# GFNet mixing and SoLU on one core: an opening stage with other places for its weights, stores, evictions and row splits

## The chip, the cores and the metric

The kernel runs on one core of one Trainium2 chip. A profile is of one execution; its span is about 2 us shorter than the device time of the same execution. The granted clock is the share of TensorE's full clock that the throttle granted in a stretch, the DMA share the mean busy share of the 16 DMA engines.

## The reference, cut to what matters

```python
# x: (8, 3136, 256)  filt_r, filt_i: (1569, 256)  w_in: (256, 1024)  w_out: (1024, 256), weights in float64
X = np.fft.rfft(x, axis=1)
y = np.fft.irfft(X * (filt_r + 1j * filt_i), n=3136, axis=1)
h = y.reshape(25088, 256) @ w_in
e = np.exp(h - h.max(-1, keepdims=True))
solu = h * e / (e.sum(-1, keepdims=True) + 1e-9)
ln = (solu - solu.mean(-1, keepdims=True)) / np.sqrt(solu.var(-1, keepdims=True) + 1e-6) * g_ln
out = ln @ w_out
```

## The kernel before

The transform over 3136 = 49 x 64 points is done in steps of matmuls with a pass through device memory between them. For the first two entries of the batch (group 0) it stands ahead of the main part, but for the last step of entry 1; this is the opening. The rest is done in pieces between the blocks of the main part, where a block is 128 tokens through both weight matrices. The first eight blocks, in which TensorE still has to wait, are called the ramp.

The opening has three parts. In the first step, 16 pieces of x (98 rows x 1024) are loaded, multiplied (`pa`), evicted (copied) from PSUM, where matmuls leave their results, to `t` and stored to device memory `d`. In the unit loop, 25 units are fetched back, multiplied (`pb`), turned and multiplied with the filter (`i`, `p`), multiplied again (`pc`), evicted (`g`) and stored. On the way back, entry 0 is fetched again and multiplied in small matmuls of 98 columns (`py`).

```python
sp = Spectrum(0, pools, resident)
for i in range(2 * NH // NCH):                      # first step: 16 pieces
    sp.fetch_x(i)                                   # one transfer of 98 rows, from SyncE
    sp.first(i, (0, 1), ..., either)                # evictions in turn on ScalarE and VectorE
    sp.store_first(i, nc.scalar.dma_start)          # one transfer of 100 rows, from ScalarE
    if i < 3:
        load_group(i)                               # tables and filters of 5 units each
...
for i in range(NS):                                 # unit loop: 25 units
    sp.multiply(i)
    if i + 1 < NS:
        start(i + 1)                                # fetch in two transfers, filter, pb
    sp.inverse(i, nc.scalar.copy if i % 3 == 0 else nc.vector.tensor_copy)
    sp.store(i, nc.scalar.dma_start)
    if i in (6, 9, 12, 15):
        load_float64(...)                           # w_in: 10 VectorE instructions each
...                                                 # w_out: four more conversions, way back
with tc.manual_schedule():
    for k in range(blocks + LAG):                   # main part, one block each
        hidden(k)                                   # h, maximum (VectorE), exponential (ScalarE)
        ...
        for job in early[k]: job()                  # pieces of other entries: pa, py, pb
        ...                                         # project, normalize (square on ScalarE)
        for job in products[k] + late[k] + stores[k] + loads[k]: job()
```

## Time and profile before

| | before |
|---|---|
| device time, median (range) | 1905.72 us (1905.46 to 1908.1) |
| span of the profile | 1902.9 us |
| first product of the unit loop | 79.8 us |
| first matmul of the way back | 174.3 us |
| first and eighth hidden layer `h` | 203.4 us, 276.5 us |

The prediction below shows the slices, the windows and the waits.

### The profile page before, as it was taken

The page shows a single profiled execution, that of the slowest core. Times are in us where ns is not written, and L with a number is a line of the kernel's source. Part 1 is how long each engine was busy: PE and PEld are TensorE (multiplying, and loading weights), DVE is VectorE, ACT ScalarE, POOL GpSimd, SP SyncE. Part 2 cuts the span into 40 slices and gives each one's busy share as a digit, 9 for nine tenths or more (in the row PEclk, how much of TensorE's full clock was granted, in tenths as well). Part 3 has the DMA queues.
Part 4 walks back from the last instruction along what each step waited for, and adds up shares of the span by engine and source line. Part 5 has one row for each costly group of instructions (what it writes and reads, how often), then busy time and mean ns, then how long its engine had stood idle before and what let it go on. Part 6 is the DMA issues. An engine that isn't in the chain of part 4 may idle for free.

```text
span 1902.9 us, 21234 instructions
## 1 busy us (share of the span) xinstructions
PE 1823.8 (96%) x6500; PEld 1168.5 (61%) x6500; DVE 1137.0 (60%) x1815; ACT 791.5 (42%) x1297; POOL 440.7 (23%) x1293
## 2 busy tenths in 40 slices
PE   6677889999999999999999999999999999999997
PEld 1224546676666666666666666667677676666665
DVE  1597445567766655566766655566666565566663
ACT  1142344554555544444545434344444334333331
POOL 2010133343334311123333211123322010110110
PEclk9686799999999999999999999999999999999999
DMA  9675279986877866575776656557675545434444
GB/s 268 214 211 188 92 226 239 241 209 174 189 194 204 200 150 149 134 170 140 166 186 148 151 137 141 137 134 177 146 178 112 119 100 117 99 86 110 96 92 100
DMA packets 320399, 300.78 MB, mean 158 GB/s; under 512 B 28625, under 2 KB 286418, under 8 KB 320288
## 3 DMA queue, kind: packets, MB, share of 16 engines
q1 hardware_dynamic: 284624, 206.69, 46.3%
q0 software_dynamic: 26704, 79.63, 14.9%
q10 hardware_dynamic: 8960, 13.11, 2.3%
q8 instruction: 53, 0.87, 0.2%
q14 instruction: 58, 0.48, 0.1%
HBM read 118.44 MB, written 81.40 MB: 105 GB/s over the span
## 4 chain that ended last, share of the span: by engine, by line
PE 88%; DVE 4%; DMA 2%; issue 1%; ACT 1%; POOL 0%; ACTq 0%; DVEq 0%; SPq 0%; POOLq 0%
PE h L396 35%; PE po L456 35%; PE py L253 6%; PE pc L226 4%; PE pb L196 4%; PE pa L169 3%; DMA d<-t 1%; DVE p L217 1%; DVE i L216 0%; DVE p L215 0%; DVE g L229 0%; DMA t<-d 0%; DVE nmax L401 0%; DMA f<-f_dram 0%; DMA raw_in<-in_moe_w_in_dram 0%
## 5 line engine op out<-in xcount | busy, mean ns | idle before, releaser
L456 PE MATMUL po<-w_out_sb,solu_t 128*128 128x256 f32 x3136 | 711.0, 380 | 4.5 <-DVE ot L464 4.5
L396 PE MATMUL h<-w_in_sb,y 128*128 128x512 f32 x1568 | 713.4, 598 | 0.0
L456 PEld LDWEIGHTS po<-w_out_sb,solu_t 128*128 128x128 f32 x3136 | 591.0, 190 | 137.7 <-issue 58.1
L396 PEld LDWEIGHTS h<-w_in_sb,y 128*128 128x128 f32 x1568 | 296.2, 192 | 317.8 <-issue 306.7
L401 DVE TENSOR_REDUCE nmax<-h 128x1 f32<-128x1024 f32 x196 | 239.6, 1222 | 419.6 <-PE h L396 419.6
L404 ACT ACTIVATE e<-h,nmax 128x1024 f32<-128x1024 f32 x196 | 218.5, 1115 | 605.0 <-DVE nmax L401 605.0
L421 ACT ACTIVATE e<-solu,nmu 128x1024 f32<-128x1024 f32 x196 | 225.0, 1148 | 287.9 <-DVE solu L419 287.9
L419 DVE SCALAR_TENSOR_TENSOR solu<-e,rsum,h 128x1024 f32<-128x1024 f32 x196 | 250.9, 1280 | 7.1 <-DVE rsum L416 0.2
L429 DVE STREAM_TRANSPOSE turn<-solu 128x1024 f32<-128x1024 f32 x196 | 241.8, 1234 | 0.0
L235 POOL DMA_DIRECT2D d<-g x152 | 93.7, 621 | 507.5 <-ACT g L229 507.4
L253 PEld LDWEIGHTS py<-wi_t,t 100*128 100x128 f32 x1024 | 146.0, 211 | 51.1 <-issue 36.0
L169 PE MATMUL pa<-x,wf_t 98*100 98x512 f32 x256 | 148.5, 687 | 25.9 <-DMA x<-in_x_dram 12.5
L253 PE MATMUL py<-wi_t,t 100*128 100x98 f32 x1024 | 145.4, 293 | 6.7 <-DMA t<-d 3.5
L448 POOL COPY rs_t<-rs 32x1 f32<-32x1 f32 x784 | 141.7, 181 | 35.7
L464 DVE TENSOR_SCALAR ot<-po,rs_t 128x256 f32<-128x256 f32 x196 | 94.4, 482 | 80.5 <-PE po L456 74.2
L215 DVE TENSOR_TENSOR p<-pb,f 128x512 f32<-128x512 f32 (+1 forms) x101 | 69.0, 684 | 120.4 <-ACT i L208 119.3
L196 PE MATMUL pb<-t,de 128*128 128x512 f32 (+1 forms) x250 | 110.9, 544 | 19.2 <-DVE p L215 10.0
L226 PE MATMUL pc<-p,de 128*128 128x512 f32 (+1 forms) x250 | 110.0, 539 | 14.9 <-DVE p L217 11.5
L442 POOL TENSOR_SCALAR rs<-var 128x4 f32<-128x4 f32 x49 | 9.3, 189 | 445.7 <-ACT e L421 443.6
L169 PEld LDWEIGHTS pa<-x,wf_t 98*100 98x100 f32 x256 | 45.7, 188 | 94.5 <-issue 59.9
L196 PEld LDWEIGHTS pb<-t,de 128*128 128x128 f32 x250 | 47.8, 198 | 78.4 <-issue 43.5
L256 ACT COPY y<-py 128x392 f32<-128x392 f32 x112 | 93.6, 836 | 5.1 <-PE py L253 5.1
(62 smaller groups left out, 868.2 us busy)
## 6 DMA issues: line engine op xcount, KB each, us to landing
solu_t<-turn SPq DMA_DIRECT2D x784, 128.0 KB
t<-d SPq DMA_DIRECT2D x64, 400.0 KB
t<-d SPq DMA_DIRECT2D x198, 128.0 KB
x<-in_x_dram SPq DMA_DIRECT2D x64, 392.0 KB
out_dram<-ot SPq DMA_DIRECT2D x196, 128.0 KB
d<-t POOLq DMA_DIRECT2D x48, 400.0 KB, 5.6
d<-g POOLq DMA_DIRECT2D x148, 128.0 KB, 3.6
f<-f_dram POOLq DMA_DIRECT2D x104, 128.0 KB, 4.3
```

The costliest lines, as they stand in the source:

```text
L169: nc.tensor.matmul(out=ps[0:NK, j], lhsT=wf_t, rhs=self.xs[i][0:NR, 2 * u:2 * u + 2, :], start=True, stop=True)
L196: nc.tensor.matmul(out=ps[:, w * j:w * j + w, :], lhsT=de[:, s + j, 0, :], rhs=t2[:, w * j:w * j + w, :], start=True, stop=True)
L226: nc.tensor.matmul(out=ps[:, w * j:w * j + w, :], lhsT=de[:, s + j, 1, :], rhs=pt[:, w * j:w * j + w, :], start=True, stop=True)
L253: nc.tensor.matmul(out=psv[:, i, :], lhsT=t4s[e, ch][:, i, cb * P:cb * P + P], rhs=wi_t, start=True, stop=True)
L396: nc.tensor.matmul(out=h[:, half, :], lhsT=y[:, c, P * t:P * t + P], rhs=w_in_sb[:, c, 512 * half:512 * half + 512], start=(c == 0), stop= ...
L401: nc.vector.tensor_reduce(out=nmax, in_=h, axis=AX.X, op=ALU.max, negate=True)
L404: nc.scalar.activation(out=e, in_=h, func=AFT.Exp, bias=nmax, accum_out=esum)
L419: nc.vector.scalar_tensor_tensor(out=solu, in0=e, scalar=rsum, in1=hs.pop(k), op0=ALU.mult, op1=ALU.mult, accum_out=nmu)
L421: nc.scalar.activation(out=e, in_=solu, func=AFT.Square, bias=nmu, scale=-float(DFF), accum_out=variances[g][:, i:i + 1])
L429: nc.vector.transpose(out=turns[g][:, :, i, :], in_=solus.pop(k).rearrange("p (f j) -> p f j", j=32))
L448: nc.gpsimd.tensor_copy(out=rss[g][32 * i:32 * i + 32, c:c + 1], in_=rs[32 * c:32 * c + 32, i:i + 1])
L456: nc.tensor.matmul(out=ps, lhsT=solu_t[:, f, :], rhs=w_out_sb[:, f, :], start=(f == 0), stop=(f == KF - 1))
```

## The change

Its intent is to shorten the opening. VectorE is relieved in the unit loop: the conversion of w_in moves into the first step, that of w_out to the way back, and evictions go to ScalarE. The stores of the loop are issued from GpSimd. A unit is one transfer instead of two. Transfers of 98 or 100 rows are cut into 96 rows and a rest of 2 or 4, so that the large part is spread over more DMA engines. In the first six blocks, pieces of the other entries stand ahead of the hidden layer instead of behind it, and the last preparation of w_out moves into the first three blocks.

```diff
+    def by_16(dmas, out, in_):
+        n = out.shape[0] // 16 * 16
+        dmas[0](out=out[:n], in_=in_[:n])
+        dmas[1](out=out[n:], in_=in_[n:])
 # loads of x, stores of the first step, loads of the way back: by_16(...) instead of one transfer
 # fetch(i), store(i) of a unit: one transfer of 128 partitions instead of two of 64
         for i in range(2 * NH // NCH):
             sp.fetch_x(i)
-            sp.first(i, (0, 1), ..., either)
-            sp.store_first(i, nc.scalar.dma_start)
-            if i < 3:
-                load_group(i)
+            sp.first(i, (0, 1), ..., nc.scalar.copy)
+            sp.store_first(i, (nc.scalar.dma_start, nc.gpsimd.dma_start))
+            if i in (1, 4, 7):
+                load_tables(i // 3)
+            if i >= 8 and i % 2 == 0:
+                load_float64(weights[(i - 8) // 2][0], load_words(weights[(i - 8) // 2][1], i))
 ...
-            sp.inverse(i, nc.scalar.copy if i % 3 == 0 else nc.vector.tensor_copy)
-            sp.store(i, nc.scalar.dma_start)
-            if i in (6, 9, 12, 15):
-                load_float64(w_in_sb[...], ...)
+            sp.inverse(i, nc.scalar.copy)
+            sp.store(i, nc.gpsimd.dma_start)
 ...
-                (early, late)[u][t].append(lambda ...: sp.first(...))
+                (first_of if t < LAG else (early, late)[u])[t].append(lambda ...: sp.first(...))
 ...                                             # the same for back(...)
         for k in range(blocks + LAG):
+            for job in first_of[k]:
+                job()
             if k < blocks:
                 hidden(k)
 ...
+            if k < 3:
+                prepare_w_out(k)
```

(The core; the layout of the tables and of the device-memory buffers follows from it.)

More of the change, by code (lines that the diff above doesn't have):

```diff
@@ L58, in dft_tables @@
     v[0, :, 0], v[1, :, 0] = 1.0, 0.0
-    wf = np.zeros((N1, 2, 2, NS, 2))
-    wi = np.zeros((2, NS, 2, N1, 2))
+    wf = np.zeros((N1, 2, NS, 2, 2))
+    wi = np.zeros((NS, 2, 2, N1, 2))
     for h in range(2):
-        wf[:, h, :, :, h] = w
-        wi[:, :, h, :, h] = v.transpose(0, 2, 1) / S
+        wf[:, h, :, :, h] = w.transpose(0, 2, 1)
+        wi[:, :, h, :, h] = v.transpose(2, 0, 1) / S
     kap = np.where(q[:, None] < 32, s + N1 * q[:, None], s + N1 * (95 - q[:, None]))
@@ L108 @@
     small = pool("sm", 4)
-    d1 = [dram.tile([len(g[0]), 2 * NS, N2, C], FP32, name=f"d1_{n}") for n, g in enumerate(GROUPS)]
-    d2 = [dram.tile([len(g[0]), 2 * NS, N2, C], FP32, name=f"d2_{n}") for n, g in enumerate(GROUPS)]
+    d1 = [dram.tile([len(g[0]), NS, P, C], FP32, name=f"d1_{n}") for n, g in enumerate(GROUPS)]
+    d2 = [dram.tile([len(g[0]), NS, P, C], FP32, name=f"d2_{n}") for n, g in enumerate(GROUPS)]
     f_dram = dram.tile([NS, NQ, 2, C], FP32, name="f_dram")
@@ L120 @@
     neg_half = consts.tile([P, 4], FP32, name="neg_half")
+    ones = consts.tile([P, P], FP32, name="ones")
+    w_bar = consts.tile([P, C], FP32, name="w_bar")
     nc.vector.memset(neg_half, -0.5)
@@ L148, in __init__, with columns @@
             self.xs, self.t1s, self.t2s, self.fs, self.prods, self.gs = {}, {}, {}, {}, {}, {}
-        def rows(self, ap, s, count, p):
+        def columns(self, ap, s, count):
             if len(self.entries) == 2:
-                return ap[:, p * NS + s, :, :].rearrange("b n c -> n b c")
-            return ap[0, p * NS + s:p * NS + s + count, :, :].rearrange("s n c -> n s c")
+                return ap[:, s, :, :].rearrange("b p c -> p b c")
+            return ap[0, s:s + count, :, :].rearrange("s p c -> p s c")
         def fetch_x(self, i):
@@ L158, in fetch_x @@
             self.xs[i] = self.pools["r"].tile([P, NCH, C], FP32, name=f"x_{self.n}_{i}", tag="r")
-            nc.sync.dma_start(out=self.xs[i][0:NR],
-                              in_=x[self.entries[b]].rearrange("(r n) c -> r n c", n=NH)[
-                                  :, NCH * ch:NCH * ch + NCH, :])
+            by_16((nc.sync.dma_start, nc.sync.dma_start), self.xs[i][0:NR],
+                  x[self.entries[b]].rearrange("(r n) c -> r n c", n=NH)[
+                      :, NCH * ch:NCH * ch + NCH, :])
         def first(self, i, halves, ps, evac):
@@ L173, in first, with store_first @@
                  in_=ps[0:NK].rearrange("p a b -> p (a b)"))
-        def store_first(self, i, dma):
+        def store_first(self, i, dmas):
             b, ch = divmod(i, NH // NCH)
-            dma(out=d1[self.n][b].rearrange("a (h n) c -> (a h) n c", h=2)[
-                :, NCH * ch:NCH * ch + NCH, :], in_=self.t1s.pop(i))
+            by_16(dmas, d1[self.n][b].rearrange("s (a n) c -> (s a) n c", a=4)[
+                :, NCH * ch:NCH * ch + NCH, :], self.t1s.pop(i))
             del self.xs[i]
@@ L184, in fetch @@
             self.t2s[i] = self.pools["t2"].tile([P, 2, C], FP32, name=f"t2_{self.n}_{i}", tag="t2")
-            for p in range(2):
-                nc.sync.dma_start(out=self.t2s[i][N2 * p:N2 * p + N2, 0:cols, :],
-                                  in_=self.rows(d1[self.n], s, count, p))
+            nc.sync.dma_start(out=self.t2s[i][:, 0:cols, :],
+                              in_=self.columns(d1[self.n], s, count))
         def fetch_filter(self, i):
@@ L233, in store @@
             gt, cols = self.gs.pop(i), len(self.entries) * count
-            for p in range(2):
-                dma(out=self.rows(d2[self.n], s, count, p),
-                    in_=gt[N2 * p:N2 * p + N2, 0:cols, :])
+            dma(out=self.columns(d2[self.n], s, count), in_=gt[:, 0:cols, :])
     t4s = {}
@@ L243, in fetch_back @@
         t4s[e, ch] = rows_pool.tile([P, NCH, C], FP32, name=f"t4_{e}_{ch}", tag="r")[0:NK]
-        nc.sync.dma_start(
-            out=t4s[e, ch],
-            in_=d2[n][b].rearrange("a (h n) c -> (a h) n c", h=2)[:, NCH * ch:NCH * ch + NCH, :])
+        by_16(
+            (nc.sync.dma_start, nc.sync.dma_start), t4s[e, ch],
+            d2[n][b].rearrange("s (a n) c -> (s a) n c", a=4)[:, NCH * ch:NCH * ch + NCH, :])
     def back(e, ch, cb, evac):
@@ L256, in back, with psum @@
         evac(out=y[:, cb, t0:t0 + S].rearrange("p (r n) -> p n r", n=NH)[:, n0:n0 + NCH, :], in_=psv)
-    flip = [0]
-    def either(out, in_):
-        flip[0] ^= 1
-        if flip[0]:
-            nc.scalar.copy(out=out, in_=in_)
-        else:
-            nc.vector.tensor_copy(out=out, in_=in_)
+    def psum(kind, name):
+        return {"b": ps_b, "t": ps_t, "o": ps_o}[kind].tile([P, 2, C], FP32, name=name, tag=kind)
     with ExitStack() as st:
@@ L271, with load_words @@
         fpool = pool("fp", 3, stack=st)
-        wpool = pool("wp", 1, stack=st)
-        def load_float64(dst, src, n):
+        wpool = pool("wp", 2, stack=st)
+        def load_words(src, n):
             raw = wpool.tile([P, 512, 2], I32, name=f"raw_{n}", tag="raw")
@@ L280, in load_float64 @@
                 in_=src)
+            return raw
+        def load_float64(dst, raw):
             lo, hi = raw[:, :, 0], raw[:, :, 1]
-            power = wpool.tile([P, 512], I32, name=f"power_{n}", tag="power")
-            frac = wpool.tile([P, 512], I32, name=f"frac_{n}", tag="frac")
+            power = wpool.tile([P, 512], I32, name="power", tag="power", bufs=1)
+            frac = dst.bitcast(I32)
             ts, stt = nc.vector.tensor_scalar, nc.vector.scalar_tensor_tensor
@@ L297, in load_float64, with load_tables @@
             stt(out=rest, in0=lo, scalar=2.0 ** -44, in1=rest, op0=ALU.mult, op1=ALU.mult)
-            nc.vector.tensor_tensor(out=dst, in0=frac.bitcast(FP32), in1=rest, op=ALU.add)
-        groups = {}
-        def load_group(g):
+            nc.vector.tensor_tensor(out=dst, in0=dst, in1=rest, op=ALU.add)
+        filters = {}
+        def load_tables(g):
             gs = slice(NG * g, NG * g + NG)
             nc.gpsimd.dma_start(out=de[:, gs, :, :], in_=de_dram[:, gs, :, :])
-            groups[g] = f = fpool.tile([P, NG, 2, C], FP32, name=f"f_{g}", tag="f")
+            filters[g] = f = fpool.tile([P, NG, 2, C], FP32, name=f"f_{g}", tag="f")
             for k, filt in enumerate((filt_r, filt_i)):
@@ L309, in load_group @@
                                         in_=filter_rows(filt, half, NG * g, NG))
-                nc.vector.tensor_copy(out=f[NQ:P, :, k, :], in_=f[0:NQ, :, k, :])
+            nc.vector.tensor_copy(out=f[NQ:P], in_=f[0:NQ])
+        weights = []
+        for c in range(KD):
+            for half in range(2):
+                hs = slice(512 * half, 512 * half + 512)
+                weights.append((w_in_sb[:, c, hs], w_in_words[P * c:P * c + P, hs]))
+        for h in range(4):
+            weights.append((w_out_sb[:, 2 * h:2 * h + 2, :].rearrange("p k d -> p (k d)"),
+                            w_out_words[256 * h:256 * h + 256].rearrange("(k p) d w -> p k d w", p=P)))
         def resident(s, count):
@@ L314, in resident, with begin @@
             if i == 0 and 1 <= g < NS // NG - 2:
-                load_group(g + 2)
-            return groups[g][:, i:i + count]
+                load_tables(g + 2)
+            return filters[g][:, i:i + count]
         sp = Spectrum(0, pools, resident)
+        raws = {}
+        def begin(j):
+            raws[j] = load_words(weights[j][1], j)
         for i in range(2 * NH // NCH):
             sp.fetch_x(i)
-            sp.first(i, (0, 1), ps_h.tile([P, 2, 512], FP32, name=f"pa_0_{i}", tag="h"), either)
-            sp.store_first(i, nc.scalar.dma_start)
-            if i < 3:
-                load_group(i)
+            sp.first(i, (0, 1), ps_h.tile([P, 2, 512], FP32, name=f"pa_0_{i}", tag="h"),
+                     nc.scalar.copy)
+            sp.store_first(i, (nc.scalar.dma_start, nc.gpsimd.dma_start))
[3 more added lines that the diff above has]
+                load_float64(weights[(i - 8) // 2][0], load_words(weights[(i - 8) // 2][1], i))
         nc.gpsimd.dma_start(out=wi_t, in_=wi_dram)
@@ L338 @@
                 start(i + 1)
-            sp.inverse(i, nc.scalar.copy if i % 3 == 0 else nc.vector.tensor_copy)
-            sp.store(i, nc.scalar.dma_start)
-            if i in (6, 9, 12, 15):
-                c, half = divmod((i - 6) // 3, 2)
-                load_float64(w_in_sb[:, c, 512 * half:512 * half + 512],
-                             w_in_words[P * c:P * c + P, 512 * half:512 * half + 512], f"in{c}{half}")
-        for h in range(4):
-            load_float64(
-                w_out_sb[:, 2 * h:2 * h + 2, :].rearrange("p k d -> p (k d)"),
-                w_out_words[256 * h:256 * h + 256].rearrange("(k p) d w -> p k d w", p=P), f"out{h}")
+            sp.inverse(i, nc.scalar.copy)
+            sp.store(i, nc.gpsimd.dma_start)
+        for j in (4, 5):
+            begin(j)
         for ch in range(NH // NCH):
@@ L351, with prepare_w_out @@
             for cb in range(KD):
-                back(0, ch, cb, either)
-        ones = wpool.tile([P, P], FP32, name="ones", tag="ones")
-        nc.vector.memset(ones, 1.0)
-        for f in range(KF):
-            nc.vector.tensor_scalar(out=w_out_sb[:, f, :], in0=w_out_sb[:, f, :],
-                                    scalar1=g_sb[:, f:f + 1], scalar2=-float(DFF), op0=ALU.mult,
-                                    op1=ALU.mult)
-        ps = ps_o.tile([P, C], FP32, name="ps_mean", tag="o")
-        for f in range(KF):
-            nc.tensor.matmul(out=ps, lhsT=ones, rhs=w_out_sb[:, f, :],
-                             start=(f == 0), stop=(f == KF - 1))
-        w_bar = wpool.tile([P, C], FP32, name="w_bar", tag="w_bar")
-        nc.scalar.mul(w_bar, ps, 1.0 / DFF)
-        for f in range(KF):
-            nc.vector.tensor_tensor(out=w_out_sb[:, f, :], in0=w_out_sb[:, f, :], in1=w_bar,
-                                    op=ALU.subtract)
+                back(0, ch, cb, nc.scalar.copy)
+        for j in range(4, 8):
+            load_float64(weights[j][0], raws.pop(j))
+            if j + 2 < 8:
+                begin(j + 2)
+    def prepare_w_out(step):
+        if step == 0:
+            nc.vector.memset(ones, 1.0)
+            for f in range(KF):
+                nc.vector.tensor_scalar(out=w_out_sb[:, f, :], in0=w_out_sb[:, f, :],
+                                        scalar1=g_sb[:, f:f + 1], scalar2=-float(DFF), op0=ALU.mult,
+                                        op1=ALU.mult)
+        elif step == 1:
+            ps = psum("o", "ps_mean")[:, 0, :]
+            for f in range(KF):
+                nc.tensor.matmul(out=ps, lhsT=ones, rhs=w_out_sb[:, f, :],
+                                 start=(f == 0), stop=(f == KF - 1))
+            nc.scalar.mul(w_bar, ps, 1.0 / DFF)
+        else:
+            for f in range(KF):
+                nc.vector.tensor_tensor(out=w_out_sb[:, f, :], in0=w_out_sb[:, f, :], in1=w_bar,
+                                        op=ALU.subtract)
     wk = pool("wk", 1)
@@ L452, in project @@
         g, a = divmod(k, 4)
-        ps = ps_o.tile([P, C], FP32, name=f"po_{k}", tag="o")
+        ps = ps_o.tile([P, 2, C], FP32, name=f"po_{k}", tag="o")[:, 0, :]
         solu_t = solu_ts.pop((g, a))
@@ L472 @@
     blocks = NT * B // 2
-    early, products, late, stores, loads = ([[] for _ in range(blocks + LAG)] for _ in range(5))
+    first_of, early, products, late, stores, loads = (
+        [[] for _ in range(blocks + LAG)] for _ in range(6))
     def spread(count, start, over):
@@ L491 @@
     row_loads = []
-    def psum(kind, name):
-        return (ps_b if kind == "b" else ps_t).tile([P, 2, C], FP32, name=name, tag=kind)
     for n in range(1, len(GROUPS)):
@@ L502 @@
             for u in range(2):
-                (early, late)[u][t].append(lambda sp=sp, i=i, u=u: sp.first(
+                (first_of if t < LAG else (early, late)[u])[t].append(lambda sp=sp, i=i, u=u: sp.first(
                     i, (u,), psum("t", f"pa_{sp.n}_{i}_{u}").rearrange("p a c -> p (a c)").rearrange(
                         "p (o n) -> p o n", o=1), nc.scalar.copy))
-            stores[t].append(lambda sp=sp, i=i: sp.store_first(i, nc.gpsimd.dma_start))
+            stores[t].append(lambda sp=sp, i=i: sp.store_first(i, (nc.gpsimd.dma_start,) * 2))
         for i, t in enumerate(spread(len(sp.units), *spectrum_at)):
@@ L519 @@
             for cb in range(KD):
-                (early, late)[cb][t].append(
+                (first_of if t < LAG else (early, late)[cb])[t].append(
                     lambda e=e, ch=ch, cb=cb: back(e, ch, cb, nc.scalar.copy))
```

## The prediction

> **What bounds the kernel now.** I read the page's slices first, to see where the bound changes. Engines, clock and DMA by slice of 47.6 us:
>
> ```profile
> PE   6677889999999999999999999999999999999997
> PEclk9686799999999999999999999999999999999999
> DMA  9675279986877866575776656557675545434444
> ```
>
> From about 300 us to the end TensorE is full at full clock, and nothing in the change removes a matmul. So what can move is the opening (the spectrum of entries 0 and 1, then the way back of entry 0) up to the first hidden-layer matmul, and the ramp of the first blocks behind it. I cut the opening into its steps with a table of windows, the borders being read from the timeline:
>
> ```profile
> 0.00:30.00 30.00, 21.00 (x25) 5.92 (x26) 6.70 (x8) 4.32 (x4) 10.74 (x21) 1.00 0.91 242
> 30.00:50.00 20.00, 12.19 (x20) 3.48 (x18) 2.76 (x4) 2.02 (x2) 1.75 (x3) 0.77 0.92 309
> 56.00:64.00 8.00, 7.93 (x10) 2.42 (x9) 3.24 (x3) 1.01 (x1) 0.00 (x0) 0.50 0.64 263
> ...
> 108.00:165.20 57.20, 41.06 (x69) 11.92 (x67) 53.29 (x95) 22.28 (x39) 4.31 (x7) 0.86 0.64 184
> 165.20:174.30 9.10, 3.22 (x8) 1.86 (x9) 5.99 (x15) 0.55 (x1) 0.70 (x1) 0.69 0.66 217
> 174.30:203.40 29.10, 29.08 (x132) 28.74 (x133) 12.82 (x24) 6.66 (x8) 0.72 (x1) 0.50 0.34 123
> 203.40:276.70 73.30, 63.59 (x167) 30.36 (x166) 31.85 (x54) 30.76 (x54) 21.17 (x48) 0.85 0.57 174
> ```
>
> Columns: stretch, length, busy us of PE, weight load, VectorE, ScalarE and GpSimd with instruction counts, granted clock, DMA share, GB/s. Up to 50 us the DMA engines are at 0.92. In 108 to 165 VectorE is busy 53.29 of 57.20 us: the unit loop (25 units) is bound by VectorE. In 174 to 203 TensorE is full, but at clock 0.50. The waits of the first step, and the groups of the loop, say why:
>
> ```profile
> ACT t L263 <- DMA d<-t: 29.9, 4, 8.7
> DVE t L265 <- DMA d<-t: 24.8, 4, 8.7
> ...
> L217 DVE TENSOR_TENSOR p<-p,i 128x512 f32<-128x512 f32 x25 | 17.1, 683 | 0.1
> L229 DVE COPY g<-pc 128x512 f32<-128x512 f32 x16 | 11.0, 689 | 5.5 <-PE pc L226 5.4
> L207 ACT ACTIVATE i<-pb 64x512 f32<-64x512 f32 x24 | 14.2, 593 | 32.4 <-DVE p L217 17.2 <-DVE i L216 7.0 <-DMA d<-g 3.9
> ```
>
> Evictions of the first step wait 55 us in sum for a buffer that the store of an earlier piece still holds. In the loop ScalarE is idle 32 us before one group alone, waiting for VectorE.
>
> **What the Trainium skill says.** "DMA: Bandwidth & Descriptors", section "Why a DMA increments its semaphore by 16 and not by 1", states that a transfer uses the largest number of engines up to 16 that divides the slowest dimension of both sides: 100 rows give 10 engines. The trace agrees: in 56 to 64 us almost only stores of 100 rows run, and the share is 0.64 with every eviction waiting for them; 98 rows would by the same rule give 14, 96 rows 16. The same page, "Rules for kernel authors", says of two transfers to disjoint partition halves that they use the same engines anyway; so one transfer per unit in place of two saves issues, not bandwidth (no run here shows that yet). "TensorE: Matmul & The Clock Gate", Part 1, says that the clock is halved by default and released by sustained activity. The trace agrees on the half, 0.50 in 174 to 203, but differs on the release: 29 us of unbroken small matmuls (98 columns) do not raise it there.
>
> **The change part by part.**
>
> *First step, row splits.* Load in KB on the busiest engines, by the rule above. Before: loads 16 x 392 / 14 = 448, stores 16 x 400 / 10 = 640, tables and weights issued in it (5 x 640, 12 x 160, 1 x 512) / 16 = 352; sum 1440 on ten engines. After: 16 x 384 / 16 = 384 for loads and the same for stores, the 2-row rests 64 on two engines, the 4-row rests about 16, and tables (3 x 640, 12 x 160, 4 x 512) / 16 = 368; sum 1152, on two engines 1216. That is 0.84 of before at worst. The first unit's fetch is issued at 72.8 us before, with transfers running from about 4; 68.8 x 0.84 = 58, so it moves to about 62. The instruction order puts the four conversions of w_in (ten VectorE instructions each, about 4.7 us at the measured pitch of 0.34 and 0.60) ahead of the first product. Their raw loads share two buffers, so the third waits for the first conversion; I estimate the fourth ends at 58 to 68, about level with the first unit. First product: 62 + 3.4 (fetch) + 2.1 (cold matmul) = 67.5, against 79.8 before, which had to finish a conversion too. Gain 12.
>
> *Unit loop.* Before, 79.8 to 163.0 (last product): 83 us. VectorE had 75 tensor operations, 16 evictions g, four filter copies, and about four conversions. After, evictions go to ScalarE and w_in's conversions are gone; the instruction order leaves in the loop 75 x 0.60 (start to start in the timeline) = 45, two copies of 64x2560 (twice the measured 0.95 each) = 3.8, and some fourteen conversion instructions of w_out = 6.3: 55 us. ScalarE: 25 x 3 x 0.60 = 45. TensorE: 25 x 4 records x 0.43 = 43 at full clock, 85 at half. DMA: 25 x 512 KB plus filters and one raw block, 14.9 MB; in 108 to 165 the engines moved 184 GB/s at share 0.64, so full would be about 287, 52 us. Four resources lie within 55; with fill and collisions I take 60. Gain 23.
>
> *Turn to the way back.* From the last product to the first matmul py took 11.3 us (last inverse, eviction, store, landing, fetch), a chain of latencies; it stays. py: 16 groups at 1.71 us at half clock = 27.4; the mean's matmuls that stood inside (about 2 us) are gone. VectorE no longer evicts, but ScalarE alone needs 16 x 0.83 = 13, and is free. The last conversions (four, 19 us) fit in these 27 on the idle VectorE. So the opening's TensorE work ends at 67.5 + 60 + 11.3 + 27.5 = 166.3, against 203.4. Gain 37.
>
> *Ramp.* Counting records of 203.4 to 400 us at their full-clock pitch (0.43 for 512 columns, 0.216 for 256, 0.108 for 98) against elapsed time, TensorE lost 17 us in 203 to 250, 4.6 in 250 to 300, 1.8 after. After: with pieces ahead of the hidden layer, TensorE has them to do while the maximum, exponential and square of the block before run, and ScalarE evicts before it blocks on the exponential. In a one-piece block this gives a period of some 6.5 us, but in two-piece blocks the two PSUM buffers still stop TensorE until the square is through. The first block's wait for the preparation of w_out (0 h at 203.4, maximum only at 212.4) is gone, but 2.6 us of the mean's matmuls come in. Net I take 6, uncertain by as much.
>
> *Issues.* One GpSimd issue is 0.62 us; 25 in 60 us is nothing. In the main part row splits add issues on SyncE and GpSimd, which are far from bound; zero.
>
> Sum: 37 + 6 = 43; 1905.7 - 43 = about 1862.
>
> **Rivals.**
> 1. *The half clock takes the loop.* If TensorE stays at 0.50, the loop is 85 us as before and only 14 to 20 us are gained: about 1888. For: 0.50 in 76 to 90 and in the way back. Against: 0.86 in 108 to 165 at a thinner load than there will be. I give it 1 in 8.
> 2. *DMA becomes the bound of the loop.* 1 KB pieces read and written at once; if the pace stays at 209 to 230 GB/s, 65 to 71 us: about 1870. For: share 0.74 in parts of the loop already. Against: slices of over 300 GB/s there. 1 in 4.
> 3. *GpSimd's order.* Its stores and rests queue behind raw loads that wait for conversions and for earlier transfers; a late rest holds the last buffer, and the loop starts at 80 as before: about 1874. For: the waits for a conversion in GpSimd's order. Against: only the last two or three pieces come after such loads. 1 in 5.
> 4. *Everything clicks.* Balanced engines finish the first step by 55, the loop is 55, and the way back enters warm (14 us rather than 27): about 1840. For: nothing but arithmetic; the 9 us pause before py is likely to cool it again. 1 in 10.
>
> **Range and chances.** The opening's gain spreads by some 10 us, the ramp's by 6; together about 12. Range 1846 to 1880. The border of 2% is 1867.6, half a spread above my figure: faster 0.67, same 0.32, slower 0.01.
>
> **What would show it.** First step: the waits of evictions for d<-t mostly gone, first unit fetched near 62 us. Loop: VectorE over 85% busy, product to product 2.2 to 2.5 us, ScalarE nearly as busy; if instead DMA is at 0.9 or more with VectorE waiting for t<-d, rival 2; if TensorE is full at clock 0.5, rival 1. Way back: again 27 us at 0.50, ending near 166. Ramp: TensorE's loss up to 300 us at 13 to 18 rather than 22. From there to the end the same length to within 2 us; if the main part changes by more, I have the wrong stage altogether.

## More of the kernel before

The metric is the device time of one execution in microseconds (us); the median of several executions is quoted, and all executions used here are marked as fast in the record (none fell in the slower state that some executions show).

One more window is needed for the comparison: the stretch behind the ramp. The columns are the stretch, its length, then busy us (and instructions) of PE, weight load, VectorE, ScalarE and GpSimd, granted clock, DMA share, GB/s.

```profile
276.50:400.00 123.50, 122.68 (x454) 79.11 (x454) 66.94 (x104) 62.29 (x105) 42.60 (x106) 1.00 0.94 240
```

TensorE is busy 122.68 of 123.50 us at full clock. From here on it sets the time, and what can be gained lies ahead of 276.5 us.

## The result, and the profile after

The changed kernel took 1884.87 us (median of 4, 1884.73 to 1890.22), the kernel before 1906.91 us in the same rounds (median of 4, 1905.46 to 1908.59). The ratio is 0.9891, with a 95% interval of 0.9871 to 0.9911. A ratio is the mean time of one kernel's fast runs over that of the other's fast runs of the same rounds, so it is not quite the ratio of the medians. The gain is 1.1%: clearly there, but below 2%, about half of the 43 us that were predicted, and outside the predicted range. It lies near the 1888 us of the prediction's first rival, but by chance: that rival's half clock in the loop did not come.

The profiled execution of the changed kernel is the slowest of its four (span 1888.3). A second profile of the same kernel (e1 below) has span 1884.2. This table has the length of each stage in both, from the timelines and the chain of work; a product is a VectorE multiplication `p`, and the loop ends where the last inverse transform `pc` starts. The last two columns are the stages that the prediction gives and the difference from e1.

| stage, us | before | after | after again (e1) | predicted | e1 less predicted |
|---|---|---|---|---|---|
| start to first product of the loop | 79.8 | 81.6 | 81.5 | 67.5 | +14.0 |
| unit loop, to the last inverse | 83.2 | 60.5 | 59.1 | 60 | -0.9 |
| turn to the way back | 11.3 | 11.5 | 10.2 | 11.3 | -1.1 |
| way back and ramp, to the eighth `h` | 102.2 | 108.9 | 107.5 | 94.6 | +12.9 |
| rest | 1626.4 | 1625.9 | 1626.0 | same | |

(102.2 is 29.1 + 73.1; the prediction's 94.6 is 27.5 and 73.1 - 6.) The loop gained what was predicted. The first step, which should have given 12 us, gave none, and the ramp lost where it should have gained.

The slices and the windows of the changed kernel, to be held against those in the prediction:

```profile
PE   6687899999999999999999999999999999999997
PEclk9695899999999999999999999999999999999999
DMA  9775579967678766656756646467674535434444
```

```profile
30.00:50.00 20.00, 9.54 (x19) 3.06 (x20) 2.98 (x2) 5.06 (x5) 7.55 (x12) 0.85 1.02 342
56.00:64.00 8.00, 7.44 (x12) 2.42 (x10) 7.28 (x17) 3.03 (x4) 2.82 (x5) 0.69 0.71 226
81.50:142.00 60.50, 48.66 (x95) 16.18 (x94) 56.94 (x94) 42.08 (x73) 23.81 (x34) 0.97 0.72 223
142.00:153.50 11.50, 1.10 (x2) 0.31 (x3) 10.52 (x23) 0.58 (x1) 2.01 (x3) 0.68 0.92 261
153.50:181.00 27.50, 27.48 (x129) 27.50 (x130) 2.65 (x4) 12.39 (x15) 0.00 (x0) 0.50 0.46 113
181.00:262.40 81.40, 69.24 (x177) 36.66 (x177) 31.92 (x59) 32.51 (x55) 24.91 (x55) 0.82 0.55 154
262.40:400.00 137.60, 137.03 (x506) 88.90 (x506) 75.69 (x116) 68.61 (x115) 49.99 (x118) 1.00 0.94 243
```

Reading down: the loop takes 60.5 us with VectorE busy 56.94 of them (94%) and the clock at 0.97. The way back is again 27.5 us at 0.50. The ramp takes 81.4 us, in which TensorE is busy 69.24. Behind it TensorE is full at full clock, as before.

Of the evictions in the first step that waited for stores (29.9 and 24.8 us before), this is left:

```profile
ACT t L180 <- DMA d<-t: 2.6, 1, 2.6
```

So most of the evictions' waits are gone, and yet the loop does not start earlier. Part of the waiting has only moved. Before, SyncE's queue (SPq), which issues the loads of x, held none of them for a store; it waited for earlier loads (30.1 us) and for TensorE (10.9). Now it waits for stores too (total us, times, longest), and TensorE waits 19.6 us for x in place of 12.5:

```profile
SPq L145 <- DMA d<-t: 17.2, 6, 4.6
```

The chain of work behind the last eviction shows the rest of the way to the loop (start, length, what):

```profile
63.48 1.02 ACT t L180
...
64.52 6.69 DMA d<-t
...
71.23 6.90 DMA t<-d
...
78.26 2.06 PE pb L203 x2
```

The last eviction ends at 64.5 us. The store then takes 6.69 us to land and the first fetch 6.90 us, where the fetch before took 3.4 (72.8 to 76.2). In e1 they take 5.19 and 9.10. In this kernel the tables of the last two groups and a block of w_out are issued right behind the last piece, and share the DMA engines with these two transfers.

The groups of the loop, as in the prediction (busy, mean ns | idle before and who ended it):

```profile
L222 DVE TENSOR_TENSOR p<-pb,f 128x512 f32<-128x512 f32 x25 | 17.2, 687 | 10.4 <-ACT i L215 8.9 <-PE pc L233 1.5
L214 ACT ACTIVATE i<-pb 64x512 f32<-64x512 f32 x24 | 14.2, 594 | 13.9 <-DVE p L224 12.0 <-PE pb L203 1.3
```

The products and ScalarE's copies now wait for each other in turn (10.4 and 13.9 us in the whole loop; VectorE fills its part with conversions), where ScalarE had waited 32.4 us ahead of this group.

### The profile page after: what moved, and what is told of

Same layout as the page of the kernel before. It is cut to its first block, busy times and chain, and to the rows that moved or that the text cites. A ratio compares the mean times of both kernels' runs of the same rounds, so it can differ in the third digit from the quotient of the medians.

```text
span 1888.3 us, 21235 instructions
## 1 busy us (share of the span) xinstructions
PE 1808.9 (96%) x6500; PEld 1169.1 (62%) x6500; DVE 1111.4 (59%) x1778; ACT 816.6 (43%) x1329; POOL 456.8 (24%) x1306
## 4 chain that ended last, share of the span: by engine, by line
PE 88%; issue 4%; DMA 4%; POOL 2%; ACT 1%; DVE 1%; SPq 0%; POOLq 0%; DVEq 0%; ACTq 0%
PE po L475 35%; PE h L415 34%; PE py L258 7%; PE pa L177 5%; PE pb L203 3%; PE pc L233 3%; DMA x<-in_x_dram 2%; POOL d L241 1%; DMA t<-d 1%; DMA d<-t 1%; DMA f<-f_dram 0%; ACT e L423 0%; DVE nmax L420 0%; DVE solu L438 0%; ACT t L180 0%
## 5 line engine op out<-in xcount | busy, mean ns | idle before, releaser
L241 POOL DMA_DIRECT2D d<-g x101 | 76.0, 753 | 567.6 <-ACT g L236 557.2
L177 PE MATMUL pa<-x,wf_t 98*100 98x512 f32 x256 | 144.6, 674 | 25.1 <-DMA x<-in_x_dram 19.6
L258 PE MATMUL py<-wi_t,t 100*128 100x98 f32 x1024 | 147.8, 297 | 17.7 <-DMA t<-d 10.4
L483 DVE TENSOR_SCALAR ot<-po,rs_t 128x256 f32<-128x256 f32 x196 | 94.5, 482 | 84.3 <-PE po L475 73.1
L203 PE MATMUL pb<-t,de 128*128 128x512 f32 (+1 forms) x250 | 106.3, 524 | 16.1 <-DMA t<-d 14.8
L261 ACT COPY y<-py 128x392 f32<-128x392 f32 x128 | 106.8, 834 | 33.1 <-PE py L258 33.0
L233 PE MATMUL pc<-p,de 128*128 128x512 f32 (+1 forms) x250 | 104.4, 516 | 10.6 <-DVE p L224 9.2
L177 PEld LDWEIGHTS pa<-x,wf_t 98*100 98x100 f32 x256 | 45.9, 186 | 90.1 <-issue 71.5
L180 ACT COPY t<-pa 100x512 f32<-100x512 f32 (+1 forms) x112 | 71.1, 640 | 69.1 <-PE pa L177 58.4
```

Source lines behind the costliest of these rows:

```text
L177: nc.tensor.matmul(out=ps[0:NK, j], lhsT=wf_t, rhs=self.xs[i][0:NR, 2 * u:2 * u + 2, :], start=True, stop=True)
L203: nc.tensor.matmul(out=ps[:, w * j:w * j + w, :], lhsT=de[:, s + j, 0, :], rhs=t2[:, w * j:w * j + w, :], start=True, stop=True)
L233: nc.tensor.matmul(out=ps[:, w * j:w * j + w, :], lhsT=de[:, s + j, 1, :], rhs=pt[:, w * j:w * j + w, :], start=True, stop=True)
L258: nc.tensor.matmul(out=psv[:, i, :], lhsT=t4s[e, ch][:, i, cb * P:cb * P + P], rhs=wi_t, start=True, stop=True)
```

## The experiments

All runs were made on four chips (e1 to e4, e5 to e8, e9 to e11, e12 to e14), on which the kernel before had medians of 1904.5 to 1906.6 us, so totals of different chips compare to 2 us or so. The position of a stage moves by several us between profiles of the same code: in five profiles whose first step is the changed kernel's (the two above, e3, e8 and e12) the last eviction starts at 59.8 to 64.6 us, the first `pb` at 73.0 to 78.8 and the first product at 76.3 to 82.1. Smaller shifts there prove nothing. The loop is steadier: 59.1 us in e1, e3, e8 and e12, 60.5 in the first profile.

### e1: the changed kernel again

No edit.

> The changed kernel again, unaltered, because its one profile fell in the longest of its four runs (1890.2 us against 1884.8). Expected 1884 to 1886 us, with the first product of the unit loop near 81 us and the first matmul of the way back near 153 us. If the stages shift by more than 2 us from the first profile, smaller differences between single profiles carry no weight.

Measured: 1885.44 us (1880.68 to 1887.51), ratio 0.9886 (0.9862 to 0.9909). The result repeats, with stages as in the table above.

### e2: no row splits in the first step

```diff
-            by_16((nc.sync.dma_start, nc.sync.dma_start), self.xs[i][0:NR], x[...])
+            nc.sync.dma_start(out=self.xs[i][0:NR], in_=x[...])        # group 0 only
-            by_16(dmas, d1[...], self.t1s.pop(i))
+            dmas[0](out=d1[...], in_=self.t1s.pop(i))                  # group 0 only
```

> Undoes the 96+rest split in the first step only: loads of 98 and stores of 100 rows in one transfer each. Theory A (the rests of 2 and 4 rows take places in the row of transfers in flight and land late, so the loads arrive in bursts and eat up what the balance gives): the first product moves forward from 81.5 to about 74 to 78 us and the total falls by 3 to 7 us against the control. Theory B (the balance works, the loss is elsewhere): evictions wait for stores again as in the kernel before, the first product moves back to 84 or later and the total rises by 3 us or more. About equal (within 2 us): split and rests cancel.

Measured: 1890.41 us, ratio 0.9917 (0.9903 to 0.9932), 5 us longer than e1, as theory B had it. Evictions wait 19.4 us for stores again, and the last one is at 69.9 us against 62.7; the loop is the same (59.4). The splits are worth 5 us in the total. The first product is at 86.3 against 81.5, but it is not the store and the fetch that hold it there: the first `pb` is at 79.8, inside 2 us of e1's, because the fetch takes only 3.0 us. Behind it VectorE stands for the raw words of w_out, as in this build 50 conversion instructions come ahead of the first product where e1 has 38. So the 5 us contain an effect of the order of instructions too.

### e3: pieces behind the hidden layer

```diff
-                (first_of if t < LAG else (early, late)[u])[t].append(...)
+                (early, late)[u][t].append(...)          # and the same for back(...)
```

> Undoes only the order of the first six blocks: pieces follow the hidden layer again. Theory C (pieces in front cost: the ramp from the last py of the way back to the eighth hidden layer took 81.5 us in the changed kernel against 73.1 before): the ramp shrinks to 74 to 77 us and the total falls by 4 to 7 us. Rival (the ramp is longer for other reasons, the mean's matmuls and late stores, and pieces in front help a little): the ramp stays at 80 us or grows, the total rises by 0 to 5 us.

Measured: 1875.74 us (1870.96 to 1879.73), ratio 0.984 (0.9813 to 0.9866), some 10 us below the changed kernel. From the end of the way back to the eighth `h` it takes 69.6 us instead of 81.4 and, in e1, 79.9 (before: 73.1). The new order, meant as a gain, is a loss. Two timelines of the changed kernel show its mechanism, TensorE's first and ScalarE's second (start, length, what, idle before):

```profile
190.90 1.88 PE L177 MATMUL pa<-x,wf_t 98*100 98x512 f32 x4
197.34 3.69 PE L258 MATMUL py<-wi_t,t 100*128 100x98 f32 x16 [4.56 <-ACT t L180]
200.83 5.33 PE L415 MATMUL h<-w_in_sb,y 128*128 128x512 f32 x8
```

```profile
195.58 1.15 ACT L440 ACTIVATE e<-solu,nmu 128x1024 f32<-128x1024 f32 x1 [2.02 <-DVE solu L438]
...
196.72 1.05 ACT L180 COPY t<-pa 100x512 f32<-100x512 f32 x2
```

The next piece's `pa` is done at 192.8, but its evictions stand behind the exponential and the square of the block before on ScalarE, and the square waits for VectorE. They come at 196.72. Both PSUM buffers are full until then, so TensorE stands 4.56 us, and the next `h` takes 5.33 us instead of 3.60: the granted clock fell to 0.50 at 197.4 us. In e3 the same place looks like this:

```profile
178.42 1.88 PE L177 MATMUL pa<-x,wf_t 98*100 98x512 f32 x4
181.61 1.96 PE L177 MATMUL pa<-x,wf_t 98*100 98x512 f32 x4 [1.31 <-ACT t L180]
183.41 3.60 PE L415 MATMUL h<-w_in_sb,y 128*128 128x512 f32 x8
```

TensorE's pause is 1.31 us, and `h` runs at 3.60 us.

### e4: tables and w_out words at other times

```diff
+            if i == 7:
+                for g in (3, 4):            # and no longer with the filters of these groups
+                    nc.gpsimd.dma_start(out=de[:, gs, :, :], in_=de_dram[:, gs, :, :])
 ...
-        for j in (4, 5):
-            begin(j)
+            if i in (4, 6):
+                begin(2 + i // 2, hold)     # held by a small copy until this unit's store
```

> Keeps everything, but loads the last two groups of the transform tables (1.3 MB) with the third, as the kernel before did, and holds the two raw weight loads of w_out (1 MB) until units 4 and 6 of the loop are stored. Theory D (these four transfers, issued right behind the last piece, slow the landing of the last stores and the fetch of the first unit, which took 6.7 and 6.9 us): the step from last eviction to first product shrinks from 17 to 12 us, the total falls by 3 to 5 us. Rival (the same bytes only move into the first step, whose loads are then later by as much): first product within 1 us of the control.

Measured: 1887.12 us, ratio 0.9897 (0.9881 to 0.9914). From the last eviction's start to the first `pb` it is 9.2 us (14.8 in the changed kernel), but the last eviction comes at 66.4 and the loop takes 65.6 us; the total is the same. So the time was moved and not won. In the loop it is not the bytes alone: VectorE is busy 60.5 us there instead of e1's 57.0, because six more conversion instructions fell into it.

### e5: evictions of the loop on both engines

```diff
-            sp.inverse(i, nc.scalar.copy)
+            sp.inverse(i, nc.scalar.copy if i % 3 == 0 else nc.vector.tensor_copy)
```

> The changed kernel with the evictions of the loop's inverse shared as before (every third on ScalarE, two of three on VectorE). If VectorE sets the loop, its 16 or 17 evictions at 0.60 add about 10 us: the loop from first product to last inverse grows from 59 us to 66 to 70, the total by 6 to 10 us against the control. Rival (the loop is set by transfers or by the chain through ScalarE, which is nearly as busy): within 2 us, or shorter.

Measured: 1891.08 us, ratio 0.9926 (0.9908 to 0.9943); the loop takes 66.6 us. In the groups, ScalarE waits for VectorE's product again:

```profile
L214 ACT ACTIVATE i<-pb 64x512 f32<-64x512 f32 x23 | 13.7, 595 | 26.3 <-DVE p L224 26.3
```

26.3 us of idle time instead of 13.9. VectorE is busy 63.6 us instead of e1's 57.0 (16 evictions more, seven conversion instructions fewer), and the loop is 7.5 us longer. VectorE sets the loop, as the prediction took it, and moving the evictions is worth 7.5 us in the loop and 5.6 us in the total.

### e6: w_in converted in the loop

```diff
-            if i >= 8 and i % 2 == 0:
-                load_float64(weights[(i - 8) // 2][0], load_words(...))
 ...
+            if i in (6, 9, 12, 15):
+                load_float64(weights[(i - 6) // 3][0], load_words(...))
```

> The changed kernel with the four conversions of w_in, and their raw loads, back in the unit loop at units 6, 9, 12 and 15. Two things are told apart: the loop should grow by 4 x 4.7 = 19 us if VectorE sets it (59 to 75-78); and the first step should shorten if the 2.1 MB of raw loads are what it lacks (last eviction from 62.7 to 57 or less, first product from 81.5 to 74-77). Total then 10 to 15 us above the control. If the first step does not move (within 2 us), the raw loads are not the reason that it fell short of the prediction.

Measured: 1889.98 us, ratio 0.9913 (0.9897 to 0.993). The loop takes 69.6 us, 10.6 more than e1's and fewer than the 16 to 19 expected. The four conversions of w_in are 40 instructions, but the loop holds only 37 conversion instructions in all, against 17 in e1, as others moved out of it. So VectorE is busy 66.0 us instead of 57.0: again the loop follows VectorE.

On the first step the run is not decisive. The last eviction is at 59.4 us, the first `pb` at 72.8 and the first product at 76.1, each just below the spread of unchanged code. Yet the total is only 4.5 us above e1 with a loop that is 10.6 longer and with later stages that are the same to within 0.7 us each; the difference is the first product, 5.4 us earlier. Whether the conversions and their loads cost the first step some 5 us stays open here; e13 asks again.

### e7: two transfers per unit

```diff
-            nc.sync.dma_start(out=self.t2s[i][:, 0:cols, :], in_=self.columns(d1[self.n], s, count))
+            for p in range(2):                # partitions 0 to 63 and 64 to 127, and so for the store
+                nc.sync.dma_start(out=self.t2s[i][h, 0:cols, :], in_=self.columns(...)[h])
```

> The changed kernel with two half-partition transfers per unit again, for fetches and stores, all through the kernel. Expected within 2 us of the control (1883 to 1888): the bytes and the rows are the same, GpSimd issues 25 more at 0.7 us in a loop where it waits for ScalarE for 30 us. Rival (the halves cost landing time or places in flight): loop and way back grow, total up by 4 us or more.

Measured: 1892.32 us, ratio 0.9931 (0.9917 to 0.9946); the loop takes 65.2 us. That is 7 us longer than e1. The expected 2 us are exceeded. But the edit also changed the order of instructions: 24 instead of 17 conversion instructions stand in the loop, and VectorE is busy 60.8 us there instead of 57.0. How much is due to the halves is not shown.

### e8: TensorE kept busy ahead of the way back

On e3's kernel, with eight matmuls (each leaves two records in the trace) in the pause ahead of the way back. Their results are not used.

```diff
+        warm = ps_o.tile([P, 2, C], FP32, name="warm", tag="o")
+        for n in range(8):
+            nc.tensor.matmul(out=warm, lhsT=de[:, n, 0, :], rhs=last, start=True, stop=True)
         for ch in range(NH // NCH):
             fetch_back(0, ch, pools["r"])
```

> The better order of the blocks (pieces behind) with eight idle matmuls of 512 columns on the last unit's tile, in the pause of about 10 us ahead of the way back; their result is not used. Theory E (the way back runs at half clock because the pause let it fall, and stays fast if it starts fast): the 128 py records take 14 to 17 us rather than 27.4, the total falls by 10 to 13 us, to about 1864. Rival (these matmuls of 98 columns do not hold the full clock): py starts fast and falls back within a few us, 23 to 27 us, total within 4 us of 1875.

Measured: 1864.25 us (1861.92 to 1874.19), ratio 0.9791 (0.9764 to 0.9818).

```profile
140.10 7.13 PE L363 MATMUL warm<-g,de 128*128 128x512 f32 x16 [0.68 <-ACT g L236]
148.83 16.49 PE L258 MATMUL py<-wi_t,t 100*128 100x98 f32 x128 [1.60 <-DMA t<-d]
```

The 128 records of the way back take 16.49 us instead of 27.60. One of the four runs (1874.19) was 10 us longer than the others, which is about this difference; its mean granted clock is 0.979 where the other three have 0.987 to 0.988, so it seems to have lost the clock on the way back.

### e9, e10, e11: what else can be taken from the first step

All on e8's kernel. e9 holds the tables of the last two groups until units 2 and 6 are stored. e10 adds 11 unused matmuls among the later pieces of the first step, to raise its clock. e11 does both.

```diff
+            if i in (2, 6):                                   # e9, e11
+                load_de(3 + i // 6, last[0:32, 0, 0:1])      # and no longer with the filters
 ...
+            for n in range({8: 3, 9: 3, 10: 5}.get(i, 0)):    # e10, e11
+                nc.tensor.matmul(out=w1[0:NK], lhsT=wf_t, rhs=sp.xs[i][0:NR, 0:2, :], ...)
```

> The kernel of e8 with the loads of the two exp tables for the turned copies' later groups held back until unit 2 and unit 6 are stored (a small copy on GpSimd makes them wait). Theory F: these 1.3 MB lie right behind the last pieces in the queues and lengthen the landing of the last store and the first fetch; the pause from the last piece's eviction to the first transpose back falls from about 15 us to about 11 us, the loop stays at 59 to 60 us, total 3 to 5 us below e8 (about 1860). Rival: the bytes only move into the unit loop, which lengthens by as much; total within 2 us of e8 (1864).

> The kernel of e8 with 11 unused 512-column matmuls among the later pieces of the first step, where TensorE stood idle for 6 us and then worked at half clock. Theory G: the last pieces run at about 1.9 us instead of 3.4 us a half, the last eviction of the first step moves from about 61 us to 57 to 58 us and the total falls 3 to 4 us below e8 (about 1861). Rival: the loads set the last pieces, or the unused matmuls at half clock only take room: last eviction at 61 us or later, total the same as e8 or up to 3 us longer.

> Both edits of e9 and e10 together on the kernel of e8. If theories F and G both hold the gains add: total 6 to 9 us below e8 (1855 to 1858), first product at about 72 us. If the first step is set by the loads alone, at most one of the two gains shows: 1860 to 1865.

Measured: 1870.99 us (1864.1 to 1873.47), 1872.12 us (1865.22 to 1878.4) and 1876.63 us (1871.66 to 1884.57), ratios 0.981 (0.9785 to 0.9835), 0.9827 (0.9794 to 0.986) and 0.9856 (0.9826 to 0.9886). None is below e8.

In e9 the time from the last eviction to the first `pb` falls from 14.9 to 10.5 us as expected, and the first product moves to 74.6. But the loop ends at 137.7, against 138.3 in e8: it is 4 us longer, as the rival had it. In e10 the clock does rise, and the later pieces run at 1.02 us for two records. But the last eviction is at 63.1: from 49.3 us on, the added matmuls took some 6 us of TensorE themselves. In e11, which does both, it is at 64.5 and the loop takes 60.6. So neither theory brought a gain.

The medians also hold a second effect. In all three profiles the way back was slow again. In e9:

```profile
139.49 7.13 PE L371 MATMUL warm<-g,de 128*128 128x512 f32 x16 [0.67 <-ACT g L236]
148.65 26.09 PE L258 MATMUL py<-wi_t,t 100*128 100x98 f32 x128 [2.04 <-DMA t<-d]
```

What differs from e8 just ahead of `py` is the pause: 2.04 us instead of 1.60. The clock was still 1.00 for 2.3 us of `py` in e9 and then 0.50. In e10 and e11 the pause was 2.62 and 2.56, and `py` took 27.60 in both. Single runs of e9 (1864.1) and e10 (1865.22 and 1868.17) have mean clocks of 0.986 to 0.990, as e8's better runs have; these are not below e8's 1861.92 to 1864.4 either.

### e12: ten matmuls ahead of the way back

```diff
-        for n in range(8):
+        for n in range(10):
```

> The kernel of e8 with 10 unused matmuls in place of 8 ahead of the way back, some 1.8 us more. In e8's profile the pause that was left was 1.60 us and the way back ran at 16.5 us; in e9 to e11 it was 2.04 to 2.62 us and the way back took 26 to 27.6 us again. Theory H: the clock is kept if the pause is under about 2 us; with 10 the pause is under 1 us, the way back takes 14 to 17 us in the profile and all runs lie together, at 1860 to 1866 us, none near 1874. Rival: it is chance, or the last unit's turn sets it; then the runs are spread over 10 us as before.

Measured: 1864.26 us (1858.6 to 1865.56), ratio 0.9767 (0.9743 to 0.9792), no run near 1874. The way back follows without a pause and is fast (window of the way back):

```profile
151.70:168.20 16.50, 16.35 (x130) 15.05 (x129) 3.52 (x6) 12.59 (x15) 0.00 (x0) 1.00 0.84 206
```

Clock 1.00 instead of 0.50. The gain of e8 is real: e12's interval lies wholly below e3's (0.9813 to 0.9866). In the seven profiles that have the added matmuls the way back is fast with pauses of 0 to 1.60 us (e8, e12, e13, e14) and slow with 2.04 to 2.62 (e9 to e11), so the bad run of e8 would fit a longer pause; it was not profiled.

### e13 and e14: bytes or the chain of transfers

Both on e12's kernel. e13 gives wrong results: with e9's held tables, three of the four loads of w_in words are left out. e14 loads x whole and keeps the split stores.

```diff
-                load_float64(weights[(i - 8) // 2][0], load_words(weights[(i - 8) // 2][1], i))   # e13
+                if i == 8:
+                    words = load_words(weights[0][1], i)
+                load_float64(weights[(i - 8) // 2][0], words)
 ...
-            by_16((nc.sync.dma_start, nc.sync.dma_start), self.xs[i][0:NR], x[...])               # e14
+            nc.sync.dma_start(out=self.xs[i][0:NR], in_=x[...])                 # group 0 only
```

> Wrong results on purpose: on e12 and e9's held tables, only one of the four blocks of w_in is loaded in the first step and converted four times, so 1.5 MB of raw words and 1.3 MB of tables are not asked for ahead of the first unit. Theory (a), the bytes set the first step: at the 3.3 us per MB that the engines took over the first 72 us of the changed kernel these 2.8 MB are 9 us; the first transpose back falls from about 76 us (73 to 78 in five runs) to about 67 us, the first product to about 70. Rival (b), the chain of transfers and the cold TensorE set it: first transpose back at 71 us as in e9 or later.

> The kernel of e12 with the x loads of the first step whole again (98 rows in one transfer), the stores split as in the change. Theory (b), the two transfers per load and SyncE's waits for landings set the first step: TensorE's idle 6 us ahead of the last pieces goes, the last eviction falls from 60 to 63 us to 57 us or less and the total is 3 to 5 us below e12. Theory (a), bytes: last eviction within the spread of 60 to 63 us, total within 3 us of e12; slightly longer if fourteen engines instead of sixteen for the loads matter.

Measured: e13 1862.82 us (2 runs), ratio 0.9768 (0.9745 to 0.9791); e14 1859.28 us (1856.76 to 1860.83), ratio 0.9748 (0.9731 to 0.9766). The chain behind the last eviction in each:

```profile
62.09 1.02 ACT t L180
...
63.13 3.23 DMA d<-t
...
66.38 4.28 DMA t<-d
```

```profile
60.33 1.02 ACT t L183
...
61.38 5.87 DMA d<-t
...
67.26 4.53 DMA t<-d
```

With three blocks of words and two tables fewer (e13), store and fetch take 7.5 us together instead of 13.6, but the last eviction stays where it was. The first `pb` is at 70.8, not at the 67 that bytes alone would give and no better than e9's 71.3, so leaving out the words of w_in adds nothing visible to holding the tables. (The 3.3 us per MB of the expectation should have been 3.6, from 277 GB/s; this changes nothing.) The total is no lower than e12's, because the loop takes 65.4 us instead of 59.1.

With x whole (e14), SyncE no longer waits for stores before it loads x, the last load of x is issued at 38.6 us instead of 51.8 (the changed kernel), and TensorE no longer waits for x ahead of the last pieces. But now the evictions wait for the stores again, and TensorE for them:

```profile
ACT t L183 <- DMA d<-t: 15.1, 6, 4.7
```

The first `pb` is at 71.9, the total 5 us below e12, and the last eviction still at 60.3. So neither theory holds as I put it: no edit brought the last eviction under 59 us. In e4, e9 and e13 the bytes issued behind the pieces lengthen the two transfers after the last eviction. There is no sign that the split of the loads pays; held against e2, which has whole loads and whole stores and its last eviction at 69.9, it is the split of the stores that pays (one profile each). Whether e14 is better than e12 is likely but not quite shown, as the intervals overlap.

e14 is the best version found. It beats the kernel before by 2.5% and the changed kernel by some 26 us.

## Why the prediction was wrong

**What held.** The loop was predicted at 60 us with VectorE over 85% busy and was 59.1 to 60.5 with 94% and more; e5 and e6 confirm that VectorE sets it (6.6 and 9.0 us more of VectorE, 7.5 and 10.6 us more of loop). The half clock did not take the loop (rival 1; clock 0.97), and DMA did not bind it (rival 2; share 0.72). The turn, the way back at 27 us and half clock, and the unchanged rest came as written. The fourth rival's warm entry came only when e8 made it.

**The step that failed first: "68.8 x 0.84 = 58, so it moves to about 62".** The first fetch was issued at 71.2 us, 9 us later. Then the fetch took 6.9 us rather than 3.4, and from `pb` to the product it took 3.3 rather than 2.1, as the copies on ScalarE come first. These 9.2, 3.5 and 1.2 are the 14 us (in e1 7.0, 5.8 and 1.2). The scaling took the load on the busiest DMA engine for what sets the whole step. Its evidence was in part the stretch of 56 to 64 us, and even there it was read too roundly: 1.75 of the 2.11 MB were stores, two of the three evictions waited for them and the third for a matmul, as TensorE was busy 7.93 of 8.00 us at half clock. Ahead of that stretch the engines were nearly full in sum already, as windows of both kernels show (before first, after second):

```profile
0.00:48.00 48.00, 33.19 (x44) 9.40 (x44) 8.93 (x10) 6.34 (x6) 12.49 (x24) 0.92 0.92 268
48.00:72.00 24.00, 15.50 (x20) 4.71 (x20) 11.48 (x16) 3.04 (x3) 0.53 (x1) 0.64 0.65 250
```

```profile
0.00:48.00 48.00, 28.56 (x44) 8.38 (x44) 3.84 (x4) 12.41 (x12) 17.84 (x32) 0.96 0.96 283
48.00:72.00 24.00, 15.25 (x20) 4.80 (x20) 16.95 (x35) 5.06 (x5) 7.65 (x12) 0.64 0.87 267
```

In the first 48 us the share had 0.92 to rise from, and GB/s per share are the same (268/0.92 = 291, 283/0.96 = 295). Balance could help only behind 48 us, where the share does rise from 0.65 to 0.87. There the changed kernel asks for more. Bytes moved in the first 80 us, before and after:

```profile
DMA packets 6764, 20.51 MB, mean 256 GB/s; under 512 B 980, under 2 KB 2110, under 8 KB 6764
```

```profile
DMA packets 7897, 22.24 MB, mean 278 GB/s; under 512 B 1584, under 2 KB 2858, under 8 KB 7896
```

1.7 MB more. My list of loads counted only three of the five tables for the changed kernel, though all five are issued ahead of the first fetch, and no block of w_out. e4, e9 and e13 show what such bytes cost: 4 to 6 us between the last eviction and the first `pb`. Moving them (e4, e9) only moved that time. e2 shows what the balance gave: a last eviction 7 us earlier and 5 us in the total. And the split of x made SyncE wait for stores (17.2 us) where the evictions had waited before; e14 undid that without an earlier last eviction.

What sets the last eviction at 59 to 65 us stays open. The bytes of x (16 x 392 KB), its stores (16 x 400 KB) and three groups of tables and filters (3 x 640 and 12 x 160 KB) are 16.9 MB and would take 60 us at 283 GB/s (an estimate from the window above), which fits; no run took these bytes away.

**The second step: "Net I take 6" for the ramp.** It was the wrong sign. The prediction saw that ScalarE would evict "before it blocks on the exponential" and feared the two PSUM buffers only in two-piece blocks. In fact the next block's pieces stand behind exponential and square of this one on ScalarE, and TensorE pauses for 4 to 5 us (4.56 and 4.41) and loses its clock each time. In addition the first eight records of `pa` run at half clock ahead of the first `h` (6.7 us). Undone, it gives 10 us (e3). The ramp of e3, 69.6 us against 73.1 before, suggests that the other parts of the change were worth 3.5 us there; the later runs with this order have 68.0 to 71.5.

**Rival 3** had the loop starting at 80 us and is nearest in effect, and the rests issued by GpSimd did land late (16 KB each, a median of 6.4 us from issue to landing). But in e13 the stores have the same rests, and the last one landed in 3.23 us, so the rests alone are not shown to be the cause; what is issued behind them counts.

## What to carry to other kernels

A busiest-engine sum predicted nothing here where the mean share of all DMA engines was 0.92 already; look at that share by stretch of time before scaling a stage by it, and count every load that is issued ahead of the transfer in question. When a wait has gone from one engine, look for it on the others, the issuing queues included. Check too what an edit does to the order of instructions: in e2, e4 and e7 conversions moved that no one had meant to move. Work put ahead of a consumer on TensorE did not help while its evictions queued behind a later-ready instruction on the evicting engine. Where a run of small matmuls starts cold behind a pause, a few unused matmuls that bridge it can be worth more than the rearrangement itself: here 10 us.

## What the Trainium skill lacked or had wrong

- "TensorE: Matmul & The Clock Gate", Part 1, has the clock released after about 3.4 us of sustained activity and taken back after an idle window of the same length. Here 27.6 us of unbroken 98-column matmuls stayed at 0.50, and the same matmuls ran in 16.5 us at 1.00 when they started at full clock (e8, e12). A pause of 2.04 us ahead of them was followed by the loss of the full clock (e9), one of 1.60 us was not (e8). One profile each, so no threshold follows.
- "DMA: Bandwidth & Descriptors", section "Why a DMA increments its semaphore by 16 and not by 1", gives the number of engines for a row count, and the trace agrees (a share of 0.64 where mostly stores of 100 rows ran). It lacks a warning that this need not say much about time when other transfers fill the rest: 0.92 to 0.96 in share and 268 to 283 GB/s is all that the first 48 us gained with the whole change.
- The same page, "Latency and other measured facts", speaks of a fixed cost of about 2 us for a DMA. It gives no figure for a transfer issued while many others are in flight: in this first step, stores of 16 KB took a median of 6.4 us from issue to landing.
